# Reordering the opening of a clustered-attention kernel: low parts to GpSimd, clears and tables later

## The chip, the cores and the metric

The kernel runs on one core of a Trainium2 chip. A core has five engines with queues of their own, which run in parallel and wait for each other through semaphores: PE (TensorE) multiplies matrices and transposes, DVE (VectorE) and ACT (ScalarE) work element by element and read what PE leaves in PSUM, POOL (GpSimd) works element by element on SBUF, and SP (SyncE) issues most DMAs. The metric is the time of one execution on the device in microseconds (us).

## What is computed

Attention in which a query sees only the keys of its own cluster, and behind it a two-level mixture of experts on the result (not touched by the change). Cut to what matters here:

```python
q_n = q / (norm(q) + 1e-06); k_n = k / (norm(k) + 1e-06)       # 4 x 8 heads, 768 rows of 64
c_n = centroids / (norm(centroids) + 1e-06)                    # 16 for each head
q_assign = argmax(einsum('bhsd,hcd->bhsc', q_n, c_n), axis=-1)
k_assign = argmax(einsum('bhsd,hcd->bhsc', k_n, c_n), axis=-1)
mask = q_assign[:, :, :, None] == k_assign[:, :, None, :]
scores = where(mask, scale * matmul(q, k.transpose(0, 1, 3, 2)), -1e9)
attn = exp(scores - max(scores)); attn = attn / (sum(attn) + 1e-09)
x = matmul(attn, v)            # then: group and expert by argmax of x @ w, relu(x @ w1) @ w2
```

## The kernel before

Numbers are kept as two float16 parts, a high part (the number times 16, rounded) and a low part (what the rounding lost), so that float16 matmuls give almost float32 results. The 32 heads are taken in pairs, since two heads of 64 fill the 128 partitions. For each pair, `load` and `loadv` fetch k, q and v; `split` has ScalarE make the high part of q or k and `lo_part` the low part, either on DVE in one instruction (L189) or, with `pool=True`, on GpSimd in two: a scaling in place (L186) and a subtraction (L187). `splitv` does the same for v. `spread` sends the parts by DMA into the operands: `A` (a head's high parts of q and k, with 16 mask rows, a row for the maximum and one of constants below) and `B` (crossed high and low parts).

`assign` multiplies the parts with the normalised centroids (`CH`, `CL`) on PE, 36 small matmuls for a pair, and DVE makes one-hot rows of the argmax in five steps. `mask_now` transposes those on PE into mask rows; for the query half ScalarE copies them (L280), for the key half DVE (L282).

Then come the scores, 9 units of 512 for each head. `coarse` computes rough scores (L304), DVE reduces them (L307), `rowmax` turns the reductions into the row maximum (L313, L315, transposes L320, copy L321). `fine` computes the exact scores (L344, L345), ScalarE takes their exponential p (L349), and GpSimd makes its low part `pl` (L351). `av` multiplies p and `pl` with V (L370, L371), five units behind `fine` (LAG). Coarse scores run up to 18 units ahead, 13 at the start.

The order of the work on each engine is fixed when the program is built: a scheduler takes the instructions in the order of the code, moved forward where an engine would be free, and `tc.issue_after` holds an instruction back behind another one. Work beside the units is put down in a table of jobs by unit number (`at(g, ...)`), which `beside(g)` runs. The opening itself, up to the first unit, is written out: parts of pair 0, assignment, masks, coarse scores of head 0, row maximum, V and pair 1, tables of the router (`R.setup`, L535 on) and of the experts (`cfg["setup"]`, L791 on), units.

GpSimd also clears things in the opening: the constant rows of eight operands `A` (two instructions each, L149 and L150) and the column of ones of four V (L152).

Of the kernel before, what the change touches and what calls it, by code (L numbers as in the profile page):

```python
# [34 lines left out]
def attention(ctx, tc, qT, kT, vr, cen, R, DEN, cfg):  # L35
# [53 lines left out]

    cn = const.tile([P, D], F32, name="cn")  # L90
# [70 lines left out]
    nc.vector.reciprocal(out=ss, in_=ss)  # L161
# [12 lines left out]
    def split(p, w, pool=False):  # L174
        x = st[p][w]
        if (p, "s") not in st:

            st[p, "s"] = sp.tile([P, 4, S], F16, name="parts")
        hi, lo = (st[p, "s"][:, i] for i in ((0, 2), (3, 1))[w])
        nc.scalar.activation(out=hi, in_=x, func=AF.Copy, scale=SQ)  # L180
        lo_part(lo, x, hi, pool)
        st[p, w] = (hi, lo)
# [90 lines left out]
    def mask_now(h, pool):  # L273

        for t, dst in ((0, QA[h]), (1, KA[h])):
# [33 lines left out]
    def rowmax(h):  # L309
# [6 lines left out]
        if h < 2:  # L316
# [4 lines left out]
            nc.scalar.activation(out=QA[h][64:OZ], in_=tp[64:OZ, :S], func=AF.Identity, scale=oscale[64:OZ], bias=obias[64:OZ])  # L321
# [142 lines left out]
    spread(0, (1,), part=(1,))  # L464
    run(rowmax(0))

    splitv(0, True)
    split(1, 1, True)
    split(1, 0, True)
    splitv(1, True)  # L470
    with tc.issue_after(last["mm"].ins), tc.issue_after(last["max"].ins):
# [3 lines left out]
        spread(1)  # L475
# [49 lines left out]
class Router:  # L525
# [9 lines left out]
    def setup(self):  # L535
# [4 lines left out]
        nc.vector.tensor_scalar(out=self.WR[:, 0], in0=wf, scalar1=WRS, scalar2=None, op0=ALU.mult)  # L540
        nc.vector.scalar_tensor_tensor(out=self.WR[:, 1], in0=wf, scalar=WRS, in1=self.WR[:, 0], op0=ALU.mult, op1=ALU.subtract)
# [12 lines left out]
        nc.gpsimd.iota(self.pay[:, :, 0], [[P, NT]], base=0, channel_multiplier=1, allow_small_or_imprecise_dtypes=True)  # L554
# [922 lines left out]
```

## Time and profile before

| | us |
|---|---|
| median of 3 runs | 773.43 (772.76 to 773.57) |
| the profiled execution | 779.35 |
| its span, first to last instruction | 777.5 |
| PE busy in the span | 736.5 (95%) |
| DVE, ACT, POOL busy | 620.1, 473.5, 474.9 |

The profile is one execution of the program. Times in it are counted from the span's start. PE, PEld (its weight loads), DVE, ACT and POOL are engines; SPq and ACTq are queues that issue DMAs. A row of the timeline names the start, the duration, the engine, the line of the kernel, the operation, and output <- input; in brackets stands the engine's idle time before it and what ended that. The granted clock is a share of TensorE's full speed of 2.4 GHz: 0.50 is 1.2 GHz.

### The profile page before, as it was taken

How to read it: one execution, taken by the hardware profiler on the slowest of the kernel's cores; microseconds unless marked ns; L12 is line 12 of the kernel's file. 1: busy time of each engine (PE TensorE's matmuls, PEld its weight loads, DVE VectorE, ACT ScalarE, POOL GpSimd, SP SyncE). 2: the span in 40 equal slices, each digit the busy share in tenths (PEclk: the TensorE clock that was granted, in tenths of full speed). 3: DMA queues.
4: the chain of work that ended last, by engine and by line, in shares of the span. 5: the costliest groups of instructions: out<-in, count | busy, mean ns of one | idle time of the engine just before them, and what ended most of it. 6: DMA issues, size and time to landing. Idle time of an engine off the chain costs nothing. (4 is left out here: it accounts for less than half of the span.)

```text
span 777.5 us, 26618 instructions
## 1 busy us (share of the span) xinstructions
PE 736.5 (95%) x11068; PEld 626.5 (81%) x11068; DVE 620.1 (80%) x1216; ACT 473.5 (61%) x928; POOL 474.9 (61%) x484
## 2 busy tenths in 40 slices
PE   4989999999999999998999889999999999999996
PEld 2667888878888788886788677788779999999896
DVE  5998978799788997989776656858679998988861
ACT  4567877778778787675788356444544435544542
POOL 8668687777787677876785325525645564454331
PEclk7699999999999999999999999999999999999998
DMA  8674524525245251230420297967677878878820
GB/s 245 161 215 120 145 81 119 163 73 154 61 127 172 63 164 48 74 125 2 138 97 16 101 327 256 284 206 220 222 245 233 268 235 259 271 254 264 265 81 33
DMA packets 78617, 128.03 MB, mean 165 GB/s; under 512 B 7668, under 2 KB 45428, under 8 KB 78489
## 3 DMA queue, kind: packets, MB, share of 16 engines
q1 hardware_dynamic: 73404, 112.63, 47.6%
q0 software_dynamic: 4928, 13.59, 4.9%
q8 instruction: 88, 1.44, 0.8%
q14 instruction: 41, 0.33, 0.1%
q10 hardware_dynamic: 156, 0.03, 0.0%
HBM read 93.41 MB, written 13.65 MB: 138 GB/s over the span
## 5 line engine op out<-in xcount | busy, mean ns | idle before, releaser
L351 POOL TENSOR_TENSOR pl<-p 128x512 f16<-128x512 f32 x278 | 288.6, 1053 | 106.9 <-ACT p L349 101.8
L307 DVE TENSOR_REDUCE mpart<-psc 128x1 f32<-128x512 f32 (+1 forms) x282 | 189.4, 682 | 32.4 <-PE psc L304 32.2
L349 ACT ACTIVATE p<-psf 128x512 f32<-128x512 f32 x288 | 170.0, 595 | 55.3 <-PE psf L345 51.2
L370 PE MATMUL pso<-V,p 128*128 128x65 f16 x1152 | 161.9, 193 | 0.0
L370 PE MATMUL pso<-V,pl 128*128 128x65 f16 x1152 | 161.5, 194 | 0.0
L371 PE MATMUL pso<-V,pl 128*128 128x64 f16 x1152 | 161.1, 191 | 0.0
L371 PE MATMUL pso<-V,p 128*128 128x64 f16 x1152 | 161.1, 191 | 0.0
L344 PE MATMUL psf<-A 82*128 82x384 f16 (+2 forms) x576 | 144.6, 276 | 3.7 <-ACT p L349 3.4
L345 PE MATMUL psf<-B 128*128 128x384 f16 (+2 forms) x576 | 144.6, 276 | 0.0
L371 PEld LDWEIGHTS <-p 128*128 128x128 bf16 x1152 | 112.7, 98 | 21.7 <-issue 0.4
L370 PEld LDWEIGHTS <-p 128*128 128x128 bf16 x1152 | 112.2, 97 | 11.0 <-issue 3.8
L304 PE MATMUL psc<-A 80*128 80x512 f16 (+1 forms) x376 | 109.3, 333 | 6.0 <-DVE mpart L307 4.4
L371 PEld LDWEIGHTS <-pl 128*128 128x128 f16 x1152 | 112.8, 98 | 0.5
L370 PEld LDWEIGHTS <-pl 128*128 128x128 f16 x1152 | 111.2, 97 | 0.3
L1027 DVE SCALAR_TENSOR_TENSOR hl<-psh,hh 128x160 f16<-128x160 f32 (+14 forms) x136 | 50.0, 370 | 54.0 <-ACT hh L1026 46.3
L1026 ACT ACTIVATE hh<-psh 128x160 f16<-128x160 f32 (+14 forms) x136 | 46.3, 347 | 63.0 <-PE psh L1024 61.8
L1024 PE MATMUL psh<-xT,wh0a 128*128 128x288 f16 (+7 forms) x512 | 75.0, 255 | 2.2 <-DVE xT L998 1.3
L1085 POOL DMA_INDIRECT out_dram<-y,ri x33 | 40.6, 1231 | 59.3 <-ACT y L1084 54.1
L986 POOL DMA_INDIRECT xg<-xbuf,ri x33 | 42.1, 1277 | 49.8 <-PE psm L996 30.4
L345 PEld LDWEIGHTS <-B 128*128 128x128 f16 x576 | 56.9, 99 | 14.1 <-issue 5.7
L1024 PE MATMUL psh<-xT,wh0b 128*128 128x272 f16 (+6 forms) x448 | 65.2, 254 | 2.0 <-DVE xT L998 0.9
L344 PEld LDWEIGHTS <-A 82*128 82x128 f16 x576 | 55.8, 98 | 12.3 <-issue 1.5
(327 smaller groups left out, 1770.7 us busy)
## 6 DMA issues: line engine op xcount, KB each, us to landing
st<-w SPq DMA_DIRECT2D x128, 512.0 KB
B<-parts SPq DMA_DIRECT2D x64, 192.0 KB
kx<-kT SPq DMA_DIRECT2D x16, 384.0 KB
qx<-qT SPq DMA_DIRECT2D x16, 384.0 KB
vx<-vr SPq DMA_DIRECT2D x16, 384.0 KB
A<-parts SPq DMA_DIRECT2D x32, 192.0 KB
xbuf<-xs SPq DMA_DIRECT2D x4, 1536.0 KB
A<-mk SPq DMA_DIRECT2D x56, 24.0 KB
```

Of the source, the lines that this page charges most:

```text
L304: last["mm"] = nc.tensor.matmul(out=pc[:, off:off + k1 - k0], lhsT=QA[h % 8][0:80, c * P:(c + 1) * P], rhs=KA[h % 8][0:80, k0:k1], start=T ...
L307: nc.vector.tensor_reduce(out=(mp[:, 0, 0:1], mp[:, :, 1], mp[:, 1, 0:1])[i], in_=pc.rearrange("p (a x) -> p a x", a=n), axis=AX.X, op=ALU ...
L344: nc.tensor.matmul(out=o, lhsT=KA[h % 8][0:82, ks], rhs=QA[h % 8][0:82, q0:q1], start=True, stop=False)
L345: nc.tensor.matmul(out=o, lhsT=KBs[h][:, ks], rhs=QBs[h][:, q0:q1], start=False, stop=True)
L349: cfg["exp"] = nc.scalar.activation(out=p32, in_=pf, func=AF.Exp, scale=QK / (SQ * SQ))
L351: lo = (nc.vector if u in (EARLY if h < 2 else DVE_LO[h % 8] if h < NH - 2 else DVE_END) else nc.gpsimd).tensor_tensor(out=pl, in0=p32, in ...
L370: nc.tensor.matmul(out=O[:, col:col + 65], lhsT=p[:, bs], rhs=vh, start=c == 0 and q == 0 and i == 0, stop=False, skip_group_check=True)
L371: nc.tensor.matmul(out=O[:, col:col + 64], lhsT=p[:, bs], rhs=vl, start=False, stop=c == NCH - 1 and i == 1, skip_group_check=True)
L986: self.got = nc.gpsimd.indirect_dma_start(out=xg[0:n].rearrange("p a d -> p (a d)"), out_offset=None, in_offset=bass.IndirectOffsetOnAxis( ...
L1024: self.mm = nc.tensor.matmul(out=ph[:, 0:M], lhsT=w[:, k, fs], rhs=xT[:, a, k], start=i == 0, stop=i == 3 * KD - 1)
L1026: nc.scalar.activation(out=hh[:, f], in_=ph[:, 0:M], func=AF.Relu)
L1027: self.ev = nc.vector.scalar_tensor_tensor(out=hl[:, f], in0=ph[:, 0:M], scalar=0.0, in1=hh[:, f], op0=ALU.max, op1=ALU.subtract)
```

## The change

In the opening, ScalarE loads the table of the square root first, with a one-element root as the first instruction, and the table of Exp behind the high part of q of pair 0. The low part of q of pair 0, still on DVE, is made behind the reciprocal of the norm. The low part of k of pair 0, and those of k and q of pairs 2 and 3, are made on GpSimd instead of DVE; those of pair 1 were there before. The constant rows of `A` are cleared just ahead of their first use, four of them among the first units; so are V's low part of pair 1 and the two sets of tables. Key masks of head 1 are copied by ScalarE. The copy that brings the row maximum of heads 0 and 1 into place is cut into two halves. Loads of pair 2 come earlier.

```diff
+    dummy = const.tile([P, 1], F32, name="dummy")
+    nc.vector.memset(dummy, 1.0)
+    nc.scalar.activation(out=dummy, in_=dummy, func=AF.Sqrt)
...
-    for i in range(8):
+    def rows(i):
         nc.gpsimd.memset(QA[i].bitcast(F32)[64:96], pairs(PSHIFT))
-        nc.gpsimd.memset(KA[i].bitcast(F32)[64:96], pairs(SQ * SQ))
-    for i in range(4):
-        nc.gpsimd.memset(V[i][:, :, :, 128:130], SQ)
+        last["row"] = nc.gpsimd.memset(KA[i].bitcast(F32)[64:96], pairs(SQ * SQ))
+
+    rows(0)
...
+            elif scalar:
+                nc.scalar.activation(out=dst[64:64 + C], in_=tp[64:64 + C, :S], func=AF.Identity, scale=-32768.0, bias=mbias[64:64 + C])
...
-            nc.scalar.activation(out=QA[h][64:OZ], in_=tp[64:OZ, :S], func=AF.Identity, scale=oscale[64:OZ], bias=obias[64:OZ])
+            for i in range(2):
+                hs = slice(i * S // 2, (i + 1) * S // 2)
+                nc.scalar.activation(out=QA[h][64:OZ, hs], in_=tp[64:OZ, hs], func=AF.Identity, scale=oscale[64:OZ], bias=obias[64:OZ])
...
+    def later(f, *a):
+        with tc.issue_after(cfg["lo"].ins), tc.issue_after(last["max"].ins):
+            f(*a)
...
-        at(pos[3], split, p1, 0)
-        at(pos[4], split, p1, 1)
+        at(pos[3], split, p1, 0, Q == 1)
+        at(pos[4], split, p1, 1, Q == 1)
...
-        at(pos[6], splitv, p0)
-        at(pos[7], splitv, p1)
+        at(pos[6], *((splitv, p0) if Q > 1 else (later, splitv, p0)))
+        at(pos[7], *((splitv, p1) if Q > 1 else (later, splitv, p1)))
...
-    split(0, 1)
-    split(0, 0)
-    dummy = const.tile([P, 1], F32, name="dummy")
-    nc.scalar.activation(out=dummy, in_=ss, func=AF.Exp)
+    split(0, 1, True)
+    with tc.issue_after(last["norm"].ins):
+        split(0, 0)
+    hi0 = st["hi"]
+    rows(1)
     spread(0, part=(0,))
     run(assign(0, ps_f.tile([P, 512], F32, name="psf")))
+    with tc.issue_after(hi0.ins):
+        nc.scalar.activation(out=dummy, in_=ss, func=AF.Exp)
     mask_now(0, (ps_o, "pso"))
     spread(0, (0,), part=(1,))
+    load(2)
+    split(1, 1, True)
+    split(1, 0, True)
+    splitv(0, True)
+    for i in range(4):
+        nc.gpsimd.memset(V[i][:, :, :, 128:130], SQ)
+    for i in range(2, 4):
+        rows(i)
+    with tc.issue_after(last["row"].ins):
+        split(2, 1, True)
+        split(2, 0, True)
     banks = itertools.cycle(((ps_c, "psc"), (ps_f, "psf")))
     for u in range(9):
         coarse(0, u, next(banks))
-    mask_now(1, (ps_o, "pso"))
+    run(rowmax(0))
+    mask_now(1, (ps_o, "pso"), True)
     spread(0, (1,), part=(1,))
-    run(rowmax(0))
-
-    splitv(0, True)
-    split(1, 1, True)
-    split(1, 0, True)
-    splitv(1, True)
+    spread(1, part=(0,))
+    loadv(2)
...
-    load(2)
-    loadv(2)
-    at(0, split, 2, 0)
-    at(1, split, 2, 1)
     R.setup()
-    cfg["setup"]()
+
+    for i in range(4):
+        at(5 + i // 2, later, rows, 4 + i)
+    at(9, later, splitv, 1, True)
+    at(11, later, R.tables)
+    at(12, later, cfg["setup"])
+    at(14, R.late)
```

`R.setup` keeps its load and DVE's clears; `R.tables` takes GpSimd's tables (one selection, nine iotas, one scaling) out of it, and `R.late` the four small DVE operations that need them or the router's weights (`WR`, `em`, `emask`).

ScalarE in the opening, before (ssc is the sum of squares of a centroid, parts the high parts; a row's line number is that of the high part, L180, or of the root, L159):

```order
L180 ACT_TABLE_LOAD
L180 ACTIVATE parts<-kx 128x768
L159 ACT_TABLE_LOAD
L159 ACTIVATE ssc<-ssc 128x1
L180 ACTIVATE parts<-qx 128x768
L180 ACTIVATE parts<-kx 128x768
L180 ACTIVATE parts<-qx 128x768
L455 ACT_TABLE_LOAD
L455 ACTIVATE dummy<-ssc 128x1
```

and now:

```order
L92 ACT_TABLE_LOAD
L92 ACTIVATE dummy<-dummy 128x1
L183 ACTIVATE parts<-kx 128x768
L162 ACTIVATE ssc<-ssc 128x1
L183 ACTIVATE parts<-qx 128x768
L471 ACT_TABLE_LOAD
L471 ACTIVATE dummy<-ssc 128x1
L183 ACTIVATE parts<-kx 128x768
L183 ACTIVATE parts<-qx 128x768
```

The root's table load stands first, that of Exp ahead of the high parts of pair 1.

DVE up to the first assignment, before (CH and CL are the parts of the normalised centroids, mx is the assignment's first step):

```order
L189 SCALAR_TENSOR_TENSOR parts<-kx,parts 128x768
L160 TENSOR_SCALAR ssc<-ssc 128x1
L189 SCALAR_TENSOR_TENSOR parts<-qx,parts 128x768
L161 RECIPROCAL ssc<-ssc 128x1
L164 TENSOR_SCALAR cn_231<-cn,ssc 128x64 x2
L170 CAST CH<-psm 64x4x16
```

and now:

```order
L163 TENSOR_SCALAR ssc<-ssc 128x1
L164 RECIPROCAL ssc<-ssc 128x1
L167 TENSOR_SCALAR cn_216<-cn,ssc 128x64 x2
L192 SCALAR_TENSOR_TENSOR parts<-qx,parts 128x768
L173 CAST CH<-psm 64x4x16
```

The low part of k has left DVE, and that of q stands behind the scaling of the centroids.

GpSimd among the first units, now (`pl` is the low part of a unit's exponential, p its number; the five rows of `pl` belong to the eighth to the twelfth unit):

```order
L358 TENSOR_TENSOR pl<-p_737 128x512
L358 TENSOR_TENSOR pl<-p_768 128x512
L358 TENSOR_TENSOR pl<-p_800 128x512
L189 TENSOR_SCALAR vx<-vx 128x768
L190 TENSOR_TENSOR V_177<-vx,V_177 128x12x64
L358 TENSOR_TENSOR pl<-p_876 128x512
L358 TENSOR_TENSOR pl<-p_913 128x512
L600 AFFINE_SELECT low<-ones 128x128
L601 IOTA desc_496 128x120
```

where before the same work stood ahead of the first unit:

```order
L186 TENSOR_SCALAR vx<-vx 128x768
L187 TENSOR_TENSOR parts<-qx,parts 128x768
L187 TENSOR_TENSOR V_174<-vx,V_174 128x12x64
L545 AFFINE_SELECT low<-ones 128x128
L547 IOTA desc_499 128x120
```

The low part of V of pair 1 stands behind the tenth `pl`, and the tables behind the twelfth, instead of ahead of the first.

## Rows read from the trace of the kernel before

**Rows 1.** The page's 40 slices of the span, 19.4 us each: PE's busy share and the granted clock, in tenths.

```profile
PE   4989999999999999998999889999999999999996
PEclk7699999999999999999999999999999999999998
```

**Rows 2.** The table of stretches: from:to, length, then busy time (and instructions) of PE, PEld, DVE, ACT and POOL, the granted clock, DMA share and GB/s.

```profile
8.00:31.90 23.90, 17.21 (x153) 11.53 (x154) 18.70 (x42) 10.99 (x16) 17.82 (x49) 0.50 0.81 218
31.90:42.40 10.50, 8.63 (x173) 7.35 (x172) 10.20 (x16) 5.83 (x9) 4.60 (x4) 0.99 0.57 128
42.40:45.70 3.30, 3.30 (x46) 2.48 (x44) 3.30 (x7) 2.18 (x3) 1.30 (x2) 0.51 0.64 160
...
39.85:41.90 2.05, 0.62 (x5) 0.17 (x4) 2.05 (x6) 0.23 (x1) 0.00 (x0) 1.00 0.95 217
...
64.01:100.00 35.99, 35.66 (x689) 29.60 (x686) 31.96 (x69) 29.16 (x58) 28.85 (x29) 1.00 0.47 131
```

**Rows 3.** What PE waited for in the first 80 us: the waiting operation and its line, what released it, us in total, times, longest.

```profile
PE psm L166 <- DVE cn L164: 4.7, 1, 4.7
PE pso L278 <- DVE st L253: 3.0, 1, 3.0
...
PE psc L304 <- DVE A L282: 1.0, 1, 1.0
```

**Rows 4.** Timeline of PE: the first fine scores behind the 18th unit of P·V.

```profile
64.03 0.22 PE L344 MATMUL psf<-A 82*128 82x128 f16 x1
```

**Rows 5.** Timeline of ACT in the opening.

```profile
4.68 0.84 ACT L180 ACTIVATE parts<-kx 128x768 f16<-128x768 f32 x1 [2.16 <-DMA kx<-kT]
5.54 1.28 ACT L159 ACT_TABLE_LOAD   x1
6.83 0.20 ACT L159 ACTIVATE ssc<-ssc 128x1 f32<-128x1 f32 x1
...
19.50 0.80 ACT L280 ACTIVATE A<-pso 16x768 f16<-16x768 f16 x1 [2.65 <-PE pso L278]
```

**Rows 6.** Timeline of DVE in the opening.

```profile
7.07 0.15 DVE L160 TENSOR_SCALAR ssc<-ssc 128x1 f32<-128x1 f32 x1 [0.46 <-ACT ssc L159]
7.80 0.96 DVE L189 SCALAR_TENSOR_TENSOR parts<-qx,parts 128x768 f16<-128x768 f32 x1 [0.58 <-ACT parts L180]
8.68 0.15 DVE L161 RECIPROCAL ssc<-ssc 128x1 f32<-128x1 f32 x1
8.87 0.48 DVE L164 TENSOR_SCALAR cn<-cn,ssc 128x64 f32<-128x64 f32 x2
9.98 0.22 DVE L170 CAST CH<-psm 64x64 f16<-64x64 f32 x1 [0.63 <-PE psm L166]
...
10.73 0.23 DVE L171 TENSOR_TENSOR CL<-psm,CH 64x64 f16<-64x64 f32 x1
12.14 0.56 DVE L246 TENSOR_REDUCE mx<-psf 128x24 f32<-128x384 f32 x1 [1.19 <-PE psf L241]
```

**Rows 7.** Timeline of POOL in the opening: two clears, two scalings, two subtractions, the first and the last of the tables.

```profile
5.30 0.41 POOL L149 MEMSET A<- 32x384 f32 x1
5.66 0.41 POOL L150 MEMSET A<- 32x384 f32 x1
...
11.57 0.83 POOL L186 TENSOR_SCALAR vx<-vx 128x768 f32<-128x768 f32 x1 [0.81 <-ACT V L222]
12.48 0.83 POOL L186 TENSOR_SCALAR kx<-kx 128x768 f32<-128x768 f32 x1
...
14.95 1.64 POOL L187 TENSOR_TENSOR parts<-kx,parts 128x768 f16<-128x768 f32 x1
...
21.62 0.29 POOL L545 TENSOR_SCALAR_AFFINE_SELECT low<-ones 128x128 f16<-128x128 f16 x1
...
24.16 0.44 POOL L565 TENSOR_SCALAR sih<-sih 128x289 f16<-128x289 f16 x1
```

**Rows 8.** The low parts on DVE (L189), before 70 us: instructions, shortest/median/longest in ns, first and last start.

```profile
L189 DVE SCALAR_TENSOR_TENSOR parts<-kx,parts x3: 949/954/1307, 5.7 to 42.6; 128x768 f16<-128x768 f32 x3
L189 DVE SCALAR_TENSOR_TENSOR parts<-qx,parts x3: 948/959/1792, 7.8 to 39.0; 128x768 f16<-128x768 f32 x3
```

**Rows 9.** Timeline of all engines from the last reduction of head 0 to its first fine scores.

```profile
23.45 0.56 DVE L282 TENSOR_SCALAR A<-pso 16x768 f16<-16x768 f16 x1
24.04 0.17 DVE L313 TENSOR_REDUCE m<-mpart 128x6 f32<-128x18 f32 x1
24.15 1.01 PE L304 MATMUL psc<-A 80*128 80x256 f16 x3 [1.02 <-DVE A L282]
24.96 0.84 PE L320 MATMUL psf<-ident,st 128*82 128x128 f16 x6
...
27.31 0.52 PE L344 MATMUL psf<-A 82*128 82x384 f16 x1
```

**Rows 10.** Timeline of POOL: the first `pl`, those behind an idle time, and fifteen in a row.

```profile
29.09 1.04 POOL L351 TENSOR_TENSOR pl<-p 128x512 f16<-128x512 f32 x1 [4.50 <-ACT p L349]
...
44.31 2.17 POOL L351 TENSOR_TENSOR pl<-p 128x512 f16<-128x512 f32 x2 [7.39 <-ACT p L349]
...
61.26 15.56 POOL L351 TENSOR_TENSOR pl<-p 128x512 f16<-128x512 f32 x15 [2.97 <-ACT p L349]
```

**Rows 11.** Timeline of ACT: the exponentials of two units that follow each other.

```profile
73.95 0.60 ACT L349 ACTIVATE p<-psf 128x512 f32<-128x512 f32 x1 [0.56 <-PE psf L345]
75.10 0.60 ACT L349 ACTIVATE p<-psf 128x512 f32<-128x512 f32 x1 [0.55 <-PE psf L345]
```

More of the change, by code (lines that the diff above doesn't have):

```diff
@@ L160, in attention @@
     nc.vector.tensor_scalar(out=ss, in0=ss, scalar1=1e-6, scalar2=None, op0=ALU.add)
-    nc.vector.reciprocal(out=ss, in_=ss)
+    last["norm"] = nc.vector.reciprocal(out=ss, in_=ss)
     cn2 = const.tile([P, 2, D], F32, name="cn2")
@@ L179, in split @@
         hi, lo = (st[p, "s"][:, i] for i in ((0, 2), (3, 1))[w])
-        nc.scalar.activation(out=hi, in_=x, func=AF.Copy, scale=SQ)
+        st["hi"] = nc.scalar.activation(out=hi, in_=x, func=AF.Copy, scale=SQ)
         lo_part(lo, x, hi, pool)
@@ L271, in mask, with mask_now @@
             nc.sync.dma_start(out=KA[h % 8][64:64 + C], in_=mk[64 + C * i:64 + C * i + C])
-    def mask_now(h, pool):
+    def mask_now(h, pool, scalar=False):
         for t, dst in ((0, QA[h]), (1, KA[h])):
@@ L474, in attention @@
         run(assign(1))
-        spread(1)
+        spread(1, part=(1,))
         mask_now(2, (ps_m, "psm"))
         mask_now(3, (ps_m, "psm"))
-    load(2)
-    loadv(2)
-    at(0, split, 2, 0)
-    at(1, split, 2, 1)
     R.setup()
-    cfg["setup"]()
+    for i in range(4):
[4 more added lines that the diff above has]
+    at(14, R.late)
     prev = []
@@ L539, in setup @@
         self.WR = const.tile([P, 2, KD, 20], F16, name="WR")
-        nc.vector.tensor_scalar(out=self.WR[:, 0], in0=wf, scalar1=WRS, scalar2=None, op0=ALU.mult)
-        nc.vector.scalar_tensor_tensor(out=self.WR[:, 1], in0=wf, scalar=WRS, in1=self.WR[:, 0], op0=ALU.mult, op1=ALU.subtract)
+        self.wf = wf
         self.ones = const.tile([P, P], F16, name="ones")
@@ L569, in setup @@
             nc.vector.memset(x, 0.0)
-        em = const.tile([4 * E, 4, E], F16, name="em4")
-        nc.gpsimd.iota(em, [[-E, 4], [-1, E]], base=0, channel_multiplier=1, allow_small_or_imprecise_dtypes=True)
-        nc.vector.tensor_scalar(out=em, in0=em, scalar1=0.0, scalar2=None, op0=ALU.is_equal)
+        self.em = const.tile([4 * E, 4, E], F16, name="em4")
         self.emask = const.tile([4 * E, E], F32, name="emask")
-        nc.vector.tensor_reduce(out=self.emask, in_=em.rearrange("p v e -> p e v"), axis=AX.X, op=ALU.max)
         self.wv = const.tile([4 * E, 2], F32, name="wv")
@@ L586, in setup, with tables, late @@
         self.lg, self.last, self.apart, self.done = {}, {}, True, -1
+    def tables(self):
+        nc, N, E, BS, NT = self.nc, self.N, self.E, self.BS, self.N // P
+        nc.gpsimd.affine_select(out=self.low, in_=self.ones, pattern=[[1, P]], compare_op=ALU.is_gt, fill=0.0, base=0, channel_multiplier=-1)
+        nc.gpsimd.iota(self.desc, [[0, 30], [-1, 4]], base=4, channel_multiplier=0, allow_small_or_imprecise_dtypes=True)
+        nc.gpsimd.iota(self.ebase, [[BS, E]], base=0, channel_multiplier=0, allow_small_or_imprecise_dtypes=True)
+        nc.gpsimd.iota(self.pay[:, :, 0], [[P, NT]], base=0, channel_multiplier=1, allow_small_or_imprecise_dtypes=True)
+        nc.gpsimd.iota(self.pv[:, :, 0], [[-1, NT]], base=NT, channel_multiplier=0, allow_small_or_imprecise_dtypes=True)
+        nc.gpsimd.iota(self.pv[:, :, 1], [[0, NT]], base=0, channel_multiplier=-1, allow_small_or_imprecise_dtypes=True)
+        nc.gpsimd.iota(self.sio, [[1, SL]], base=0, channel_multiplier=0, allow_small_or_imprecise_dtypes=True)
+        nc.gpsimd.iota(self.sih, [[1, SL + 1]], base=0, channel_multiplier=0, allow_small_or_imprecise_dtypes=True)
+        nc.gpsimd.tensor_scalar(out=self.sih, in0=self.sih, scalar1=1.0, scalar2=-0.5, op0=ALU.mult, op1=ALU.add)
+        nc.gpsimd.iota(self.em, [[-E, 4], [-1, E]], base=0, channel_multiplier=1, allow_small_or_imprecise_dtypes=True)
+        nc.gpsimd.iota(self.evec, [[0, 1]], base=0, channel_multiplier=1, allow_small_or_imprecise_dtypes=True)
+    def late(self):
+        nc, wf, em = self.nc, self.wf, self.em
+        nc.vector.tensor_scalar(out=self.WR[:, 0], in0=wf, scalar1=WRS, scalar2=None, op0=ALU.mult)
+        nc.vector.scalar_tensor_tensor(out=self.WR[:, 1], in0=wf, scalar=WRS, in1=self.WR[:, 0], op0=ALU.mult, op1=ALU.subtract)
+        nc.vector.tensor_scalar(out=em, in0=em, scalar1=0.0, scalar2=None, op0=ALU.is_equal)
+        nc.vector.tensor_reduce(out=self.emask, in_=em.rearrange("p v e -> p e v"), axis=AX.X, op=ALU.max)
     def blank(self):
```

12 lines of the change are left out of this document (1 added, 11 removed).

## The prediction

> **What bounds the kernel now.** I read the page's slices first, then the table of stretches, then what PE waits for in the first 80 us, then each engine's timeline there. The slices [rows 1] show PE full everywhere except at the two ends; the granted clock is 0.7, 0.6 and 0.9 of full speed in the first three slices. The stretches [rows 2] say it in numbers: from 64 to 100 us PE is busy 35.66 of 35.99 us at full clock, so behind 64 us an instant won or lost on PE stays won or lost. Ahead of it two things cost time. From 8 to 31.9 us PE is busy 17.2 of 23.9 us, all of it at 0.50, which is the 1.2 GHz level; and from 31.9 to 42.4 us DVE is busy 10.20 of 10.50 us while PE is short of work, 0.62 of 2.05 us at the end of it, after which the clock falls to half again until 45.7. The waits of PE [rows 3] name the links: 4.7 us for the normalised centroids, 3.0 for the one-hot assignment, 1.0 for a mask half on DVE.
>
> PE's work is the same in both kernels, and by the order its sequence is the same too from one point on: the end of the 18th unit of P·V (one unit is 512 scores of one head; the 24th unit of fine scores comes next). Before, that matmul starts at 64.03 [rows 4]. What the change wins there it wins at the end, so I work out when it gets there.
>
> **The change, part by part.**
>
> *Root's table.* ScalarE's table load at 5.54 takes 1.28 us and holds the root, which starts at 6.83 [rows 5]. Now the table is loaded while ScalarE waits for k, and the next ACTIVATE is the root, at some 5.55: 1.28 us sooner. The load for Exp stays, behind the high part of q, where only later parts of k and q wait for it.
>
> The Trainium skill (ScalarE: Activation LUTs, What ACT_TABLE_LOAD costs) counts about 2.66 us for a switch, load and drain together; by that the root would come 2.66 us sooner and s below would be 1.4 larger. The trace disagrees: the root started 0.01 us behind the load's end, and 1.28 holds.
>
> *Low parts of pair 0.* Before, DVE did the low part of q (7.80, 0.96 us) between the root and the reciprocal, so that the centroids were scaled only at 8.87 [rows 6]. Now the reciprocal comes first. Root done at 5.75 instead of 7.03, then 0.04 and twice 0.19 as in the rows: scaling at 6.2 instead of 8.87, 2.7 us sooner. But the low part of q now stands between the scaling and the copies of the centroids (9.98 before, so 7.3 now): it runs from 6.65 to 7.6 and pushes the last of those copies from 10.96 to 8.6. The low part of k moves to GpSimd: a scaling (0.91 from start to start) once ScalarE's high part is done, at 5.6, a clear (0.36), a subtraction (1.64 [rows 7]): done at 8.5 if nothing is in its way.
>
> Something may be. The subtraction on GpSimd and the low part on DVE both read two tensors, and in the trace the latter takes 0.95 us alone but up to 1.79 beside GpSimd's subtractions [rows 8]. They are due within 0.3 us of each other: DVE is through with the scaling at 6.65, GpSimd with its clear at 6.87. The assignment's matmuls end 1.2 us behind their last operand (10.96 to 12.14 [rows 6]). If DVE starts first, k is late, at 9.2, and the assignment ends at 10.4 instead of 12.14; if GpSimd does, DVE's copies end at 10.4 and the assignment at 11.6; if they don't meet, it ends at 9.8. I take the first, since DVE is due a little earlier. So s, by which all that follows is earlier, is 1.7 (0.55 to 2.3).
>
> The Trainium skill (SBUF — State Buffer, Who interferes with whom) calls that port an exclusive lock: the second to start waits for the whole instruction. The 1.79 fits that. By that rule nothing between the three cases is possible.
>
> *A mask half on ScalarE.* DVE's half at 23.45 delayed the row maximum to 24.04, and PE's next coarse scores waited 1.02 us for it [rows 9]. ScalarE takes some 0.8 us for it, as for the other half at 19.50 [rows 5], and is through with it at 22.6 - s, behind two high parts of pair 2. PE then goes on at 23.15 - s, as soon as it has the second assignment behind it, and its transposes at 24.0 - s instead of 24.96. The first fine scores come at 27.31 - 0.95 - 1.7 = 24.65. The row-maximum copy in two halves is worth nothing: PE is still on coarse scores then.
>
> *Five low parts leave DVE* (k of pair 0, k and q of pairs 2 and 3, and the router's small operations come later). Between 28 and 44 us that is four times 0.95 to 1.79 us, out of a stretch where DVE was the bound [rows 2, 8]. PE's idle time there, some 1.9 us, and the half clock behind it, worth 1.65 of 3.3 us, should go.
>
> *GpSimd pays.* A low part costs it 0.91 + 1.62 us, against 0.95 on DVE. What stands ahead of its first unit: six such pairs (15.2 us), six clears, the ones of V: 17.6 us from 5.6 on, 24.4 with 1.2 of waits. It does its first `pl` 1.78 us behind the first fine scores (27.31 to 29.09 [rows 9, 10]), so at 26.4: those are hidden. Behind it are queued, among the units: k and q of pair 3 and V of pair 1 (three of 2.53), eight clears (2.9), the tables (21.62 to 24.60 [rows 7]: 3.0). A `pl` is 1.04 us (15 in 15.56 [rows 10]). So the 13th is done at 26.4 + 7.6 + 2.9 + 2.4 + 13.5 = 52.8, and the 19th at 59.7. DVE's two low parts of V meet it: 0 to 1.9 us, and I take 0.5 by the 13th: 53.3.
>
> PE needs 1.15 us a unit [rows 11]. It is up with GpSimd at the tenth `pl`, and then has to wait while GpSimd does V of pair 1 and the tables: eight us for three units that PE does in 3.5. So P·V of the 13th unit runs at 53.3. Up to the shared point come five more units of P·V and some 7.2 us of PE work in all (six units at 1.15 and a transpose): 60.5. Against 64.03 that is 3.5 us.
>
> *The clock.* PE waits about 2.4 and 2.0 us in that place. The one such place before, 2.05 us at 0.62 busy, was followed by 3.3 us at the 1.2 GHz level [rows 2]. One more such stretch costs 1.65 us, part of it while PE waits for GpSimd anyway. I take 1.2 (0 to 3.3).
>
> *At nothing:* SP's queue. The load of the fourth V no longer waits for V of pair 1, but that of the fifth does, at some 48 us, and with it two loads and the eight mask copies; coarse scores of head 4 need those at some 56 us. If that cover goes, each us is one of PE's. DVE's compare for the router waits for its table on GpSimd until 51, with coarse reductions behind it; the two score banks cover it, since PE waits for the 13th `pl` until 53.3.
>
> **Sum.** 3.5 - 1.2 = 2.3 us. The profiled execution took 779.35 us (span 777.5, 1.85 around it) and would take 777.05. The median of the runs shown is 773.43, which is 0.992 of it: 771.2.
>
> **Rivals.**
>
> *GpSimd keeps up.* If PE's waits for it are short (the two low parts of V don't collide, ScalarE hands over earlier) and the clock holds, only PE's own path counts: 2.65 at the first fine scores, 1.9 of idle time, up to 1.65 of half clock: 4 to 6 us, some 768.4. For it: GpSimd stood idle 7.39 us at one place in this stretch before [rows 10]. Against it: the sum of its queue leaves no idle time from 26.4 to the 13th `pl`.
>
> *The opening wins little.* GpSimd's subtraction goes first, s is 0.55, the first `pl` moves to 27.5 and all behind it: 2.3 - 1.15, and with 0.9 more from the collisions with V's low parts nothing is left: 773.2. For it: the two are due 0.3 us apart. Against: q is a little ahead.
>
> *Slower.* PE stands still for GpSimd's backlog, loses the full clock twice, and comes back at 1.2 GHz into a stretch where it is again the bound. Price: two stretches of 3.3 us at half clock, 3.3, and DVE's compare, stuck behind the tables on GpSimd, holds the coarse reductions, 1 to 2 us: 4.3 to 5.3 against 3.5, so 774.6. It decides from the point where these cost over 3.5. Where elementwise work belongs, the Trainium skill (GPSIMD Engine Reference, Engine selection) is on its side: it puts such work on VectorE, GpSimd being about half as fast with two inputs. The rows agree (1.62 against 0.95).
>
> **How the numbers follow.** The forecast has 0.50, with its own range 769.8 to 772.5; GpSimd keeping up 0.18, little won 0.19, slower 0.13. A measurement of this kernel tells 0.2%, 1.55 us, from no change. Faster by more: 0.43 of the forecast's 0.50 and all of the first rival, with a little of the second: 0.62. Within it: the rest of the forecast and most of the second: 0.25. Slower: 0.13. The range leaves out the far ends of the outer rivals: 768.3 to 774.2.
>
> **What would show it.** The root at about 5.6 and no table load ahead of it; the first assignment's end near 10.4; the first fine scores near 24.7; no stretch of DVE at 97% between 28 and 42 us; GpSimd without a gap from 26.4 to 53; PE waiting for `pl` or behind it near 47 and 52, with the half clock after it; the 24th unit of fine scores near 61.7. The forecast is wrong if PE never waits for GpSimd there, if it waits elsewhere (on a mask copy or on DVE's compare), or if the shared point is gained and lost again behind 64 us.

## The result and the profile after

The changed kernel is slower: 781.64 us median of four runs (778.63 to 782.62) against 773.25 for the kernel before, a ratio of 1.0097 with a 95% interval of 1.0071 to 1.0122. The forecast was 771.2 us, in a range of 768.3 to 774.2.

The profiled executions are not the typical ones: 778.63 us (span 776.8) is the lowest of the four runs of the changed kernel ("after" from here on), and the profiled 779.35 us of the kernel before lies above all its timed runs. So I compare places in the traces instead of whole times. The start of a unit is the start of its first fine scores in PE's timeline (L344 before, L351 after), in us:

| unit of fine scores | 1 | 7 | 11 | 16 | 20 | 24 | 48 | 288 (last) | end of span |
|---|---|---|---|---|---|---|---|---|---|
| before | 27.31 | 42.32 | 46.80 | 51.85 | 60.32 | 64.03 | 95.77 | 422.56 | 777.5 |
| after | 27.02 | 38.03 | 43.56 | 49.98 | 64.64 | 70.91 | 102.55 | 428.76 | 776.8 |

At the seventh unit the change is 4.3 us ahead, at the 24th 6.9 behind, and it stays 6.2 to 6.9 behind to the last unit. Behind that, before took 354.9 us and after 348.0; the 18 other traces of this study have 348.0 to 353.8 there, with a median of 350.4. So the trace of before is the longest of all in its last part, by some 4.5 us over that median, and that of after one of the shortest, which hides the loss when the two profiled times are compared. Added to the median of before, the opening's 6.9 us give 780.1 (779.5 with the 6.2 that are left at the last unit) of the measured 781.64; the remaining 1.5 to 2.2 us have no place that I can show.

The slices of the page and the table of stretches of after, columns as in [rows 1, 2]:

```profile
PE   5887999999999999999899899999999999999996
PEclk7698999999999999999999999999999999999999
```

```profile
8.00:31.90 23.90, 17.54 (x148) 11.39 (x148) 16.37 (x32) 12.22 (x18) 18.52 (x23) 0.51 0.98 229
31.90:42.40 10.50, 9.99 (x173) 8.12 (x172) 9.04 (x16) 7.47 (x13) 10.10 (x12) 0.97 0.48 115
42.40:45.70 3.30, 3.30 (x82) 2.84 (x79) 3.20 (x7) 1.71 (x4) 3.16 (x6) 1.00 1.03 227
...
50.70:58.40 7.70, 5.68 (x68) 4.02 (x66) 5.91 (x8) 3.77 (x6) 7.70 (x32) 0.78 0.66 211
58.40:63.20 4.80, 0.03 (x1) 0.03 (x1) 4.80 (x4) 0.00 (x0) 3.85 (x4) 0.65 0.29 65
63.20:70.90 7.70, 7.70 (x109) 6.03 (x109) 5.85 (x11) 4.96 (x10) 4.16 (x4) 0.77 0.12 32
```

From 31.9 to 45.7 the loss of [rows 2] is gone: PE is busy 13.29 of 13.80 us at nearly full clock. Then comes a hole that was not there before: from 58.4 to 63.2 PE does almost nothing (0.03 us), ScalarE nothing, and the next 7.7 us run at a mean granted clock of 0.77. What PE and GpSimd waited for in the first 80 us, columns as in [rows 3]:

```profile
POOL pl L358 <- ACT p L356: 9.9, 7, 4.2
...
PE psc L309 <- DVE mpart L312: 5.5, 3, 4.8
...
PE psf L325 <- ACT st L320: 2.3, 1, 2.3
...
PE pso L377 <- POOL pl L358: 1.5, 1, 1.5
```

Two of PE's waits are new and large: 4.8 us for a coarse reduction (`mpart`, L312) and 2.3 us for the row maximum's copy (`st`, L320). Where the 4.8 us arise is seen in DVE's timeline, with GpSimd's beside it:

```profile
55.18 1.56 DVE L616 TENSOR_SCALAR em<-em 64x64 f16<-64x64 f16 x1 [1.79 <-POOL em L609]
56.61 0.67 DVE L312 TENSOR_REDUCE mpart<-psc 128x2 f32<-128x512 f32 x1
57.21 5.13 DVE L615 SCALAR_TENSOR_TENSOR WR<-wf,WR 128x80 f16<-128x80 f32 x1
62.27 0.24 DVE L617 TENSOR_REDUCE emask<-em 64x16 f32<-64x64 f16 x1
62.44 0.67 DVE L312 TENSOR_REDUCE mpart<-psc 128x1 f32<-128x512 f32 x1
```

```profile
57.23 5.01 POOL L358 TENSOR_TENSOR pl<-p 128x512 f16<-128x512 f32 x5
64.74 1.04 POOL L358 TENSOR_TENSOR pl<-p 128x512 f16<-128x512 f32 x1 [2.49 <-ACT p L356]
```

`em` is the router's compare. WR here and below is the second half of the router's weights (L615), 80 columns wide. In the kernel before it took 0.54 us:

```profile
31.06 0.54 DVE L541 SCALAR_TENSOR_TENSOR WR<-wf,WR 128x80 f16<-128x80 f32 x1
```

After the change it starts with a run of five subtractions on GpSimd and ends 0.1 us behind the last of them. The coarse reduction queued behind it is what PE waits for. The 2.3 us come from ScalarE, in its timeline of the opening, to be held against [rows 5]:

```profile
4.65 0.84 ACT L183 ACTIVATE parts<-kx 128x768 f16<-128x768 f32 x1 [1.90 <-DMA kx<-kT]
5.40 0.20 ACT L162 ACTIVATE ssc<-ssc 128x1 f32<-128x1 f32 x1
...
20.15 0.89 ACT L285 ACTIVATE A<-pso,mbias 16x768 f16<-16x768 f16 x1
23.40 0.84 ACT L225 ACTIVATE V<-vx 128x768 f16<-128x768 f32 x1 [2.35 <-DMA vx<-vr]
24.15 0.21 ACT L320 ACTIVATE st<-m 128x6 f16<-128x6 f32 x1
```

The row maximum is ready at 21.64 (DVE's row of L318 starts at 21.47 and takes 0.17), but its copy (`st`, L320) stands behind the high part of V of pair 2, and that waits for its load until 23.40.

### The profile page after: what moved, and what is told of

Same layout as the page of the kernel before. It is cut to its first block, busy times and chain, and to the rows that moved or that the text cites. A ratio compares the mean times of both kernels' runs of the same rounds, so it can differ in the third digit from the quotient of the medians.

```text
span 776.8 us, 26638 instructions
## 1 busy us (share of the span) xinstructions
PE 736.1 (95%) x11068; PEld 626.6 (81%) x11068; DVE 619.2 (80%) x1211; ACT 475.1 (61%) x931; POOL 494.7 (64%) x494
## 5 line engine op out<-in xcount | busy, mean ns | idle before, releaser
L312 DVE TENSOR_REDUCE mpart<-psc 128x1 f32<-128x512 f32 (+1 forms) x282 | 189.7, 681 | 34.4 <-PE psc L309 33.9
L356 ACT ACTIVATE p<-psf 128x512 f32<-128x512 f32 x288 | 170.3, 596 | 66.7 <-PE psf L352 58.4
L351 PE MATMUL psf<-A 82*128 82x384 f16 (+2 forms) x576 | 145.2, 277 | 3.5 <-ACT p L356 3.5
L1057 ACT ACTIVATE hh<-psh 128x160 f16<-128x160 f32 (+14 forms) x136 | 46.6, 346 | 64.1 <-PE psh L1055 63.5
L1116 POOL DMA_INDIRECT out_dram<-y,ri x33 | 45.1, 1367 | 60.1 <-ACT y L1115 54.6
L1017 POOL DMA_INDIRECT xg<-xbuf,ri x33 | 43.7, 1323 | 44.9 <-PE psm L1027 26.9
L351 PEld LDWEIGHTS <-A 82*128 82x128 f16 x576 | 55.9, 98 | 12.1 <-issue 1.6
```

The source lines that it names most:

```text
L312: nc.vector.tensor_reduce(out=(mp[:, 0, 0:1], mp[:, :, 1], mp[:, 1, 0:1])[i], in_=pc.rearrange("p (a x) -> p a x", a=n), axis=AX.X, op=ALU ...
L351: nc.tensor.matmul(out=o, lhsT=KA[h % 8][0:82, ks], rhs=QA[h % 8][0:82, q0:q1], start=True, stop=False)
L356: cfg["exp"] = nc.scalar.activation(out=p32, in_=pf, func=AF.Exp, scale=QK / (SQ * SQ))
L1057: nc.scalar.activation(out=hh[:, f], in_=ph[:, 0:M], func=AF.Relu)
L1116: d = nc.gpsimd.indirect_dma_start(out=self.out, out_offset=bass.IndirectOffsetOnAxis(ap=idc, axis=0), in_=y[0:n], in_offset=None, bounds_ ...
```

## The experiments

There are four theories of the loss. A: DVE's operations that share a way into SBUF with GpSimd are locked out while subtractions follow each other there. B: GpSimd's own backlog holds PE, whatever DVE does. C: ScalarE's wait of 2.35 us took the opening's gain away. D: the low part of V of pair 1, done late, frees the buffer of a later V late, and SP's queue, ScalarE and DVE wait for that load. The batches ran on different chips, so ratios are compared, each to the kernel before on its own chip. The starts of units and the time that WR took are from the profiled execution, in us; that is one execution, so they go with the ratio only roughly. (Those of v1_wr, tables_early, router_early and tables24 were the slowest of ten runs each; the two traces of the changed kernel itself differ by 1.7 us at the 24th unit.)

| kernel | 1st | 7th | 16th | 20th | 24th | WR | ratio (95%) |
|---|---|---|---|---|---|---|---|
| after | 27.02 | 38.03 | 49.98 | 64.64 | 70.91 | 5.13 | 1.0097 (1.0071 to 1.0122) |
| after_again | 27.46 | 38.17 | 50.41 | 65.06 | 72.63 | 5.13 | 1.0106 (1.0079 to 1.0133) |
| wr_early | 27.24 | 39.55 | 50.49 | 63.04 | 68.38 | 0.99 | 1.0070 (1.0044 to 1.0096) |
| v1_early | 26.76 | 37.12 | 49.26 | 61.91 | 68.32 | 5.13 | 1.0052 (1.0030 to 1.0075) |
| v1_wr | 27.11 | 40.35 | 50.00 | 58.61 | 65.06 | 0.99 | 0.9989 (0.9976 to 1.0001) |
| tables_early | 27.36 | 37.44 | 49.73 | 56.99 | 66.33 | 0.95 | 0.9985 (0.9962 to 1.0008) |
| router_early | 26.91 | 39.56 | 50.97 | 60.64 | 68.07 | 0.99 | 1.0009 (0.9986 to 1.0032) |
| act_order | 23.89 | 34.42 | 46.10 | 60.75 | 65.41 | 1.60 | 1.0017 (0.9998 to 1.0035) |
| act_wrlate | 25.21 | 35.25 | 47.41 | 61.26 | 66.09 | 0.23 | 1.0017 (0.9999 to 1.0035) |
| v1_act | 24.20 | 37.45 | 49.19 | 56.94 | 61.60 | 1.13 | 0.9955 (0.9941 to 0.9969) |
| v1_act_wrlate | 24.95 | 35.24 | 47.14 | 55.15 | 59.98 | 0.22 | 0.9970 (0.9947 to 0.9992) |
| v1_act_router | 26.58 | 40.94 | 51.43 | 57.62 | 63.31 | 1.25 | 0.9993 (0.9978 to 1.0008) |
| v1_act_dve23 | 25.05 | 39.73 | 50.81 | 58.19 | 63.72 | 1.06 | 0.9991 (0.9974 to 1.0009) |
| tables24 | 25.94 | 37.10 | 49.16 | 55.79 | 60.51 | 0.91 | 0.9993 (0.9970 to 1.0015) |

**The changed kernel again** (no edit).

> The changed kernel once more, unaltered, beside the kernel before, so that the other runs of this batch have both beside them. If the profile of the result is typical, PE's long wait between the 19th and the 20th unit (4.81 us behind DVE's 5.13 us) stands at the same place and the 24th unit of fine scores is near 70.9; the ratio to the kernel before is 1.007 to 1.012. If DVE's 5.13 us was a chance event of one execution, the 24th unit comes 3 us or more earlier, and the loss has another place.

It repeats to 0.01 us: WR takes 5.13 us, and PE waits 4.8 behind it. It was no chance event.

**WR alone, V alone, both.**

```diff
 # wr_early
-    (in R.late)  nc.vector.tensor_scalar(out=self.WR[:, 0], ...); nc.vector.scalar_tensor_tensor(out=self.WR[:, 1], ...)
+    (in R.setup) the same two
 # v1_early
-    at(9, later, splitv, 1, True)
+    splitv(1, True)        # behind splitv(0, True)
 # v1_wr: both
```

> Changed kernel, with the two DVE operations on the router's weights (WR) put back ahead of the units; GpSimd's tables and DVE's compare stay late. Theory A (DVE is locked out for as long as GpSimd's subtractions follow each other without a gap): WR's second half takes under 1.9 us, PE's wait of 4.81 us behind it and the half clock after it go, the 24th unit of fine scores moves from 70.9 to 64 to 65.5, the time falls by 5 to 7 us to 774.5 to 776.5. Theory B (GpSimd's own backlog holds PE, DVE's long operation only lies beside it): PE waits for pl at the same place, the 24th unit stays behind 68.5, the time falls by under 2.5 us.

> Changed kernel, with GpSimd's low part of V of pair 1 put back ahead of the units. Theory D (that low part frees the buffer that V of pair 3 is loaded into; done at 50.6 it holds that load, the loads queued behind it on SP, and through them ScalarE and DVE): SP issues the load of V of pair 3 before 27 us instead of 37 and that of pair 5 near 45 instead of 52, no engine waits over 1 us for a load of V between 40 and 60 us, GpSimd's queue among the units is 2.5 us shorter, and the time falls by 3 to 6 us against the changed kernel. Theory B (GpSimd's backlog alone): PE gets the 2.5 us of GpSimd's time back and no more. Theory A (DVE's lock-out by the gapless subtractions): with GpSimd still behind at unit 14, DVE's operation on the router's weights stays over 3 us and the time falls by under 2.5 us.

> Changed kernel, with V's low part of pair 1 and the router's weights (WR) both back ahead of the units; ScalarE's wait at the first row maximum stays. Each alone gained 1.8 us (WR, 779.92) and 5.2 us (V, 776.53). Theories A and D are two stalls of which each stands behind the other: together they gain more than the sum, since PE's 4.81 us behind WR go without V's load taking their place: 24th unit of fine scores at 62 to 63.5, 770.5 to 773 us. If the two are one and the same stall (the same microseconds counted twice), the time stays at 776.

With WR moved, A's gain of 5 to 7 us did not come: the ratio fell by 0.3 to 0.4% (2 to 3 us), and the 24th unit started at 68.38. PE stood still just as long, at another place. ScalarE's timeline of wr_early, and the longest wait of PE from 40 to 72 us:

```profile
55.09 0.84 ACT L225 ACTIVATE V<-vx 128x768 f16<-128x768 f32 x1 [4.57 <-DMA vx<-vr]
55.84 0.19 ACT L320 ACTIVATE mh<-m 128x6 f16<-128x6 f32 x1
```

```profile
PE psm L333 <- ACT mh L320: 4.7, 1, 4.7
```

SP issued that load of V at 52.05, after 7.5 us of waiting for GpSimd's low part of V of pair 1 (done at 52.02). That is D, standing behind A. In v1_early SP's loads go out at 25.39 and 45.13 and nobody waits for one; A is untouched there, WR taking 5.13 us and PE waiting 4.8. Both edits together reach 0.9989, 1.17% below after_again, where the single ones gave 0.36 and 0.54%: the excess of 0.27% is about as wide as the intervals, so that they add up is shown, that they do more is not. The 24th unit, at 65.06, missed the 62 to 63.5 expected for that. With V early in both, moving WR is worth 0.63% (1.0052 to 0.9989, 4.9 us), which is PE's wait of 4.8; with WR early in both, moving V is worth 0.81% (6.3 us). That V early gains anything with A still in place fits B (2.5 us less in GpSimd's queue) as well as D.

**The tables and the whole router early.**

```diff
-    at(11, later, R.tables)
-    at(12, later, cfg["setup"])
+    R.tables(); cfg["setup"]()     # behind R.setup(); router_early: R.late() as well
```

> Changed kernel, with GpSimd's tables put back ahead of the units, where GpSimd was idle from 24.6 to 28.8 us; DVE's operations of the router stay behind unit 14. Theory A: GpSimd's queue among the units is 3.2 us shorter; if that leaves gaps between its subtractions by unit 14, DVE's WR is short and the 24th unit comes at 62 to 64 (772 to 774 us); if it leaves none, WR is long again (over 3 us) and the 24th unit stays near 68 (778 us). Theory B: PE gets just the 3.2 us of GpSimd's time back, the 24th unit at 67.7, 778 us, whatever WR takes.

> Changed kernel, with the whole of the router's preparation put back ahead of the units: GpSimd's tables and DVE's four operations. Theory A: both the backlog of 3.2 us and the lock-out go; 24th unit at 61.5 to 63.5, 771.5 to 773.5 us, level with the kernel before or faster. Theory B: 24th unit at 67 to 68, 777 to 778 us.

The ratio fell by 1.1% (tables) and 0.9% (all): 7 to 9 us, more than the 3.2 us of GpSimd's work, so B alone is out. D shows in tables_early as well: PE waits 2.1 us there for a mask copy on SP's queue. But A in the form in which I had put it is hurt too: in tables_early GpSimd is still without a gap, and WR, which starts inside its run, is short:

```profile
51.67 10.05 POOL L358 TENSOR_TENSOR pl<-p 128x512 f16<-128x512 f32 x10
```

```profile
51.86 0.95 DVE L615 SCALAR_TENSOR_TENSOR WR<-wf,WR 128x80 f16<-128x80 f32 x1
```

**ScalarE's order.**

```diff
+    last["mh"] = nc.scalar.activation(out=QA[h][64:OZ, hs], ...)      # the row maximum's copies
-    with tc.issue_after(cfg["lo"].ins), tc.issue_after(last["max"].ins):
+    with tc.issue_after(cfg["lo"].ins), tc.issue_after(last["max"].ins), tc.issue_after(last["mh"].ins):
 # act_wrlate: WR's second half held behind em besides
```

> Changed kernel, with ScalarE's high parts of V held behind head 0's row-maximum copies, so that no wait for V's load stands ahead of them. Theory C (that wait took the opening's gain away): the first fine scores come at 24.5 to 25 instead of 27.02, GpSimd's first pl at 26.5 instead of 28.8, and all behind it 2.3 us sooner: 776 to 779.5 us. If the lock-out of DVE sets the end alone (theory A without C), the first fine scores move as well, but WR's long wait stays and the time falls by under 1 us.

> Changed kernel with ScalarE's wait removed as in the run that held the high parts of V (776.02), but with WR's second half held where it was, behind DVE's compare: in that earlier run the scheduler had also moved WR to 31.8 us, so two things were changed. Theory C alone is then worth the 2.3 to 3 us by which the first fine scores and GpSimd's subtractions come earlier, and WR's stall stays: 777.5 to 780 us. If ScalarE's wait explains all of the earlier gain, the time is 776 again.

C holds as to the place: the first fine scores come at 23.89 and 25.21, and the copy of the row maximum waits for its operand only:

```profile
21.49 0.23 ACT L320 ACTIVATE st<-m 128x6 f16<-128x6 f32 x1 [0.84 <-DVE m L318]
```

The second run was to part C from WR's place, since the scheduler had moved WR in the first. It gave the same ratio, but WR fell into a stretch without subtractions (0.23 us), so A was absent in both, and neither run gives C's price by itself. In both, D stands at the end: ScalarE waits 5.95 and 6.05 us for V.

**C and D, and what is left.** v1_act is v1_early with ScalarE's order; the others change one thing in it (v1_act_dve23 puts WR ahead of the units besides).

```diff
 # v1_act_wrlate: WR's second half held behind em
 # v1_act_router: R.tables(), cfg["setup"]() and R.late() behind R.setup()
 # tables24: at(24, later, R.tables); at(25, later, cfg["setup"]); at(27, R.late)
 # v1_act_dve23 (WR ahead of the units)
-    split(2, 1, True); split(2, 0, True); at(pos[3], split, p1, 0, Q == 1); at(pos[4], split, p1, 1, Q == 1)
+    at(0, split, 2, 0); at(1, split, 2, 1); at(pos[3], split, p1, 0); at(pos[4], split, p1, 1)
```

> As the last, and ScalarE's high parts of V of pairs 2 and 3 held behind head 0's row-maximum copies. Theories C and D together: first fine scores at 23.9 as in the run that held them alone, GpSimd without the wait for V's load, 24th unit at 60 to 63 us, and 770 to 773 us, below the kernel before. If the queue of GpSimd among the units sets the end whatever stands ahead of it, the 24th unit stays at 65 and the time at 774 to 776 us.

> The best kernel so far (769.68) with one edit: WR's second half held behind DVE's compare near 54 us, where GpSimd does five subtractions without a gap. Theory A: the operation, 0.54 us in the kernel before and 1.1 at 35 us, takes 2.5 to 5.2 us there, ending with the last of the subtractions; DVE's coarse reductions behind it and PE wait, the 24th unit comes 2 to 6 us later and the time is 772 to 776. If DVE gets its turn between two subtractions, it takes under 2.1 us and the time rises by under 1 us.

> As the last, and the router's tables and DVE's four operations ahead of the units too, so that only the low parts of pair 3 and eight clears are left of GpSimd's extra work among the units. Theories A and B: 2 to 3 us below the last one. If the tables then delay GpSimd's first subtraction (it is busy to 27 us by the sum: six low parts, clears, V's and tables), the first of P.V waits and the gain is under 1 us or negative.

> The best kernel so far (769.7), with GpSimd's tables behind the 24th unit instead of the 12th and DVE's compare behind the 27th. If GpSimd's backlog near the 11th unit still costs (PE waits 1.6 us there for a subtraction), the 24th unit comes at 60 or before instead of 61.6, and the time falls by 1 to 2 us, to 768 to 769 (ratio 0.993 to 0.9945). If the backlog is hidden or moves to a later unit, the time is within 1 us of 769.7.

> The best kernel so far with the low parts of k and q of pairs 2 and 3 back on DVE, as in the kernel before (WR ahead of the units). If the part of the change that gains is what leaves DVE between 28 and 44 us, the seventh unit of fine scores goes from 37.5 back to 40 or later and the time rises by 1.5 to 4 us, to 771 to 773.5. If GpSimd's load is what still costs, the 24th unit comes earlier than 61.6 and the time falls below 769.

v1_act beats both kernels: 769.68 us, 0.9955. The scheduler put WR at 35.4 in it (1.13 us), so it lacks A, C and D. Against v1_wr, which lacks A and D alone, it gains 0.34% (2.6 us, the intervals do not overlap): that is the nearest to a price of C, and close to the 2.35 us of ScalarE's wait. Its 24th unit, at 61.60, is 0.1 from the 61.7 of the forecast, but that is luck: V's low part of pair 1, 2.53 us of the forecast's queue on GpSimd, no longer stands in that queue here. Its stretches:

```profile
31.90:42.40 10.50, 10.24 (x165) 8.07 (x163) 8.59 (x16) 7.06 (x12) 10.01 (x15) 0.89 0.78 175
42.40:50.00 7.60, 7.29 (x146) 5.92 (x142) 7.56 (x17) 3.64 (x7) 7.60 (x16) 1.00 0.56 187
50.00:61.60 11.60, 10.52 (x180) 8.18 (x177) 11.32 (x21) 9.15 (x19) 11.09 (x28) 1.00 0.46 135
```

No hole is left; PE's longest wait in these stretches is 0.7 us, for a coarse reduction. v1_act_wrlate missed its aim: WR came to stand among GpSimd's small clears, took 0.22 us, and the ratio is that of v1_act within the intervals. Low parts of pairs 2 and 3 back on DVE cost 0.36%, 2.8 us, and the seventh unit goes from 37.45 to 39.73: that is the part of the change that pays. The router early costs 0.38%: GpSimd, with the tables ahead of its low parts, does its first subtraction of a unit 3.0 us later, and the first fine scores come 2.4 us later, since DVE's compare waits for GpSimd's table with the first row maximum behind it:

```profile
23.54 0.19 DVE L616 TENSOR_SCALAR em<-em 64x64 f16<-64x64 f16 x1 [2.03 <-POOL em L609]
```

Tables behind the 24th unit won 1.1 us at that unit and had lost 4.1 again by the 31st, since the compare waited for the table once more, with a later row maximum behind it:

```profile
ACT mh L320 <- DVE m L318: 3.1, 1, 3.1
...
DVE em L616 <- POOL em L609: 1.5, 1, 1.5
```

**When is DVE locked out?** Theory A in two forms: by A1 DVE is locked out as long as GpSimd's subtractions follow each other, wherever in the run it starts; by A2 the moment of its start decides. The test is v1_early, with DVE's order kept and WR pushed into GpSimd's run by clears right ahead of it.

```diff
+    for i in range(n):       # nud_0: none; nud_2, nud_6: 2 and 6 of one column; nud_s1, nud_s2: 1 and 2 of 64x192
+        m = nc.vector.memset(..., 0.0)
+    with self.tc.issue_after(m.ins):
         nc.vector.scalar_tensor_tensor(out=self.WR[:, 1], in0=wf, scalar=WRS, in1=self.WR[:, 0], ...)
```

> Control: the kernel with V's low part of pair 1 put back (776.53 before), its order of DVE kept, with an unused small tile added. WR's second half takes 5.1 us again, PE waits 4.8 us for the coarse reduction behind it, ratio to the kernel before 1.003 to 1.0075. If it takes under 2 us here already, the long duration hangs on a start that differs by less than the rows show from run to run.

> As the control, with two clears of one column on DVE right ahead of WR's second half: it starts 0.1 to 0.2 us later, inside GpSimd's first subtraction of the run. Theory A1 (locked out as long as the subtractions follow each other without a gap): 4.9 us, ending with the run, the time as the control. Theory A2 (the operation loses its turn again and again only where it starts a few hundredths ahead of GpSimd; in the middle of a subtraction it gets the next turn): 0.9 to 1.5 us, PE's wait of 4.8 us is gone, the 24th unit of fine scores comes 4 to 6.5 us earlier, and the time is 4 to 6 us below the control.

> As the last, with six clears: it starts 0.4 to 0.6 us into the run. Theory A1: 4.5 us, the time as the control. Theory A2: under 1.1 us and the time as the last one's.

> As the control nud_0, with one longer clear (64x192, 0.2 us, of a tile that is zero already) on DVE right ahead of WR's second half: it starts 0.2 to 0.35 us into the first subtraction of GpSimd's run. Theory A1 (locked out for the whole run, whenever it starts in it): 4.8 us or as long as the run, PE's wait of 4.7 us stays, time as the control (1.002 to 1.005). Theory A2 (the moment decides, with the border between 0.14 and 0.19 us): 0.75 to 1.1 us, ending 0.06 us into the second subtraction; the 24th unit of fine scores comes 4 us or more earlier, ratio 0.997 to 1.000.

> As the last, with two such clears; by the order DVE also does the low part of head 0's output (from PSUM) ahead of WR's second half, which then starts 0.7 to 1.2 us into the run. Theory A1: until the run's end, 3.5 us or more. Theory A2: by its place in the subtraction: under 1.1 us if it starts more than 0.19 us into one, to the run's end if it starts within 0.15 us of one's start.

| kernel | WR starts, us after GpSimd's run | subtractions in the run | WR, us | 24th unit | ratio (95%) |
|---|---|---|---|---|---|
| after | -0.02 | 5 | 5.13 | 70.91 | 1.0097 (1.0071 to 1.0122) |
| nud_0 | 0.09 | 5 | 5.03 | 67.75 | 1.0023 (0.9999 to 1.0046) |
| nud_2 | 0.11 | 5 | 5.02 | 68.15 | 1.0044 (1.0018 to 1.0069) |
| nud_6 | 0.14 | 6 | 5.97 | 67.60 | 1.0047 (1.0024 to 1.0070) |
| nud_s1 | 0.30 | 6 | 5.82 | 68.14 | 1.0085 (1.0057 to 1.0113) |
| nud_s2 | 0.81 | 7 | 6.30 | 69.78 | 1.0066 (1.0039 to 1.0092) |

A2 is out: the start was moved by 0.8 us and WR ended with the run each time, the longer the run the later. (nud_6 started earlier than meant, at 0.14 instead of 0.4 to 0.6; nud_s1 and nud_s2 are the runs that decide. That nud_s1 is slower than was expected of A1, 1.0085 for 1.002 to 1.005, is not explained.) In nud_s1:

```profile
53.15 5.82 DVE L625 SCALAR_TENSOR_TENSOR WR<-wf,WR 128x80 f16<-128x80 f32 x1
58.89 0.55 DVE L398 TENSOR_TENSOR xs<-pso,xs 128x384 f16<-128x384 f32 x1
```

```profile
52.85 6.02 POOL L358 TENSOR_TENSOR pl<-p 128x512 f16<-128x512 f32 x6
```

So A1 holds for WR in eight profiles, at the same place in each. As a rule it fails: WR was short in tables_early, the compare in v1_act and wr_early (0.87 us each, inside runs of five and four), and these are not the only ones. WR met a run of five subtractions in wr_early, v1_wr, router_early and v1_act_dve23 too, 0.08 to 0.15 us behind its start, and ended with the first of them, after 0.99 to 1.06 us. In wr_early:

```profile
29.15 0.99 DVE L565 SCALAR_TENSOR_TENSOR WR<-wf,WR 128x80 f16<-128x80 f32 x1
```

```profile
29.01 5.03 POOL L358 TENSOR_TENSOR pl<-p 128x512 f16<-128x512 f32 x5 [4.78 <-ACT p L356]
```

One thing sorts all cases. Before 80 us the twenty traces have 62 DVE operations (scalings, compares, subtractions) on SBUF alone that start beside a GpSimd instruction that reads SBUF and has another such right behind it. In 19 of them that is the first of a run that begins without a pause behind a clear or an index fill (IOTA) of GpSimd: all 19 last to the end of the run, the eight long WR among them. The other 43 got in behind one instruction at the latest, in runs of up to eleven. No run was made to test this, so whether the start of the run is the cause is open.

## Why the prediction was wrong

**Right.** The root started at 5.40 (forecast 5.55). DVE's low part of q came first and GpSimd's low part of k late, as chosen: it was done at 9.06 (9.2), and the first assignment's reduction started at 10.16 (10.4). The row maximum came 2.57 us earlier. DVE's stretch at 97% and the half clock behind it are gone: the seventh unit starts 4.3 us earlier, the largest gain, and undoing the move of these low parts costs 2.8. GpSimd worked without a wait from 28.80 to 62.24. PE waited for a subtraction at 50.9, for 1.5 us (forecast near 47 and 52). That the opening's state carries to the end holds to 0.7 us over 264 units.

**Wrong, 9.2 us at the 24th unit (70.91 for 61.7).** Three terms.

First, the step "the first fine scores come at 24.65": 27.02, 2.4 late. I had followed the row maximum through DVE and PE, and counted what a moved load passes on SP and GpSimd, but not what the moved load of V holds up on ScalarE. With the wait taken out they came at 23.9 to 25.2. GpSimd started its subtractions later by the same 2.4, and its backlog began there.

Second, the 13th subtraction at 53.3: it was done at 56.66, 3.4 late. Of this 2.4 are the first term, and 0.8 more contention with DVE's two low parts of V than the 0.5 I took: beside them a scaling took 1.43 us instead of 0.83, and two subtractions 2.76 instead of 2.04.

Third, and largest: from the 13th subtraction to the shared point I had 7.2 us and 1.2 for the clock; it took 14.25. The step that failed is the sentence on DVE's compare, costed at nothing because the two score banks cover it. The compare itself waited 1.79 and took 1.56; behind it WR took 5.13, the coarse reduction behind that came late, and PE stood still for 4.81 us and came back at a granted clock of 0.50. The two banks did not cover that. I had bounded a DVE operation beside GpSimd by one subtraction, from the 1.79 of [rows 8], and WR itself had no term. In the trace of before that bound held for WR, which ended 0.1 us behind the first of two subtractions; behind the late tables and clears it stayed out for the whole run.

The other entry at nothing, SP's queue, fails as well, behind the first: once WR is out of the way PE waits 4.7 us for a load of V (wr_early).

The rival that I called slower (0.13) named this place and these means: GpSimd's backlog, two stretches of lower clock, DVE's small operations holding the coarse reductions. It priced the last at 1 to 2 us, so it gave 774.6, where the runs gave 781.64. Its direction was right and its price too low; my weight had gone to a cover that I had not checked against the order of DVE.

The sum also leaned on one trace of before, whose last part was some 4.5 us longer than the middle one of the others. That did not decide, as the same last part was taken for both.

## What to carry to other kernels

When work is moved onto an engine that then never pauses, look for every operation of another engine that shares a way into memory with it, and for what stands behind that operation. Cost it by one instruction as the usual case and by the whole run as the worst; here the worst came true eight times at one place. When a load is issued later, list what stands behind its consumer on each engine in order, not only behind the load on its queue. Stalls at the end of an opening stand behind each other: taking one out showed the next (WR, then V's load), and only pairs of edits told what each was worth.

## What the runs showed of the hardware

DVE can lose its turn for a whole run of GpSimd's subtractions: WR took 5.02 to 6.30 us in eight profiles with runs of five to seven. In eight others it met a run of two or more and got its turn behind one instruction (0.54 to 1.25 us, ending 0.1 us behind it), and beside clears alone it took 0.22 to 0.23. The Trainium skill (SBUF — State Buffer, Who interferes with whom) has the port held for the whole instruction; the short cases agree, the eight long ones show more than that.

The granted clock of the opening differs from trace to trace: in v1_early the stretches of 8 to 24 and 24 to 32 us stand at 1.00, in after at 0.52 and 0.50. It shows little in the whole time. In the batch of after_again, the kernel before had a mean granted clock under 0.985 in 13 runs, with a median of 773.11 us, and above it in 12, with 773.45; in the batch of wr_early the medians were 776.74 (15 runs) and 774.71 (14). That the means differ because of the opening is not shown, as each batch has the clock of a run only as a whole.
